# First gate and up columns ahead on ScalarE's queue, parameters behind x on SyncE

## The chip, the cores and the metric

The kernel runs on one core of one Trainium2 chip. The metric is the device time of one execution in microseconds (us). The core has four compute engines, TensorE (PE), VectorE (DVE), ScalarE (ACT) and GpSimd (POOL), and SyncE (SP), which here only issues DMAs. ScalarE can issue DMAs too. DMAs issued by SP and by ScalarE go through two queues onto the same 16 DMA engines.

## What is computed

The input x has 2048 tokens of 512 features, in bf16. It is normalised, and two blocks work on the result xn: a diagonal complex state-space layer and a gated feed-forward layer. Their sum with x is the output.

```python
xn  = layernorm(x)                                  # over the 512 features
dt  = exp(log_dt);  Lam_bar = exp(dt * (Lambda_re + 1j * Lambda_im))
Bu  = xn @ (((Lam_bar - 1) / Lam)[:, None] * (B_re + 1j * B_im)).T
h_t = Lam_bar * h_(t-1) + Bu_t                      # 2048 steps, 512 complex states
ssm = 2 * real(h @ (C_re + 1j * C_im).T) + xn * Dskip
ffn = (gelu(xn @ w_gate) * (xn @ w_up)) @ w_down    # 1376 hidden columns
out = x + ssm + ffn
```

The three parameter vectors log_dt, Lambda_re and Lambda_im have 512 values each.

## The kernel before

The tokens are worked in four blocks of 512, and a block in four tiles of 128 tokens. For each block TensorE multiplies the normalised, transposed tokens (XNT) with the gate and up columns (GU, L788), with B (BU, L731), and later adds up the feed-forward and state-space outputs (DN, L861 and L872). VectorE does the scan of the recurrence (CHAIN, L770) and much of the elementwise work; ScalarE does the gelu and takes results out of PSUM.

Instructions are not emitted in the order of the program text. Every operation is recorded with the tiles that it reads and writes, an estimated duration and an engine; a planner (`Sched.schedule`) then orders VectorE, ScalarE and GpSimd by due times. TensorE and SP keep the order in which operations are recorded. Operations handed to `S.pin` keep the order in which they are pinned, ahead of all others of their engine. Waits on semaphores follow from the tiles read and written, and from `after`.

The first block has a start of its own, and the change lies there:

- **Loads.** SP issues the four x tiles of the first block one by one (L494), then Lambda_re and Lambda_im, then the second piece of the gate and up columns (`ld_gu(1)`, columns 256 to 383), then B by two transposing DMAs (L483), then the rest. ScalarE issues log_dt, the first 256 gate columns and the first 256 up columns (L490 to L492), before it loads its first function table.
- **Parameters.** The tile PRMT is [128 x 128]: rows 0 to 3 hold log_dt, rows 4 to 7 Lambda_re, and from row 8 Lambda_im; `ld_param` (L473) repeats Lambda_im over rows 8 to 31. VectorE zeroes rows 32 to 63 and 64 to 127 by two memsets (L522, L523). One transpose on TensorE (`TR_par`, L631) turns the whole tile, so every row must hold numbers. It waits for all three parameter loads. ScalarE reads its result (L669 to L675).
- **Normalisation.** For each of the four tiles VectorE takes statistics (L538, L539), ScalarE or GpSimd forms the inverse root (L573 and L574, or L558 and L559), and VectorE centres and scales (L567 in three pieces for tile 0, L554 for the others). The order on VectorE is pinned: statistics of tiles 0 and 1, centring of tiles 0 and 1, statistics of tiles 2 and 3, centring of tiles 2 and 3.
- **TensorE.** Warm-up matmuls on constants (L890), the transposes of tile 0 (L597), the gate pieces of tile 0, the transposes of tile 1, the last gate piece (L621), then the up pieces of tile 0 and both for tile 1 (L621), the parameter transpose, and the third column group with tiles 2 and 3 (L788, L597, L621). ScalarE copies the transposes out of PSUM (L607). After these comes BU of block 0 (L731).

```python
S.pin(*st[0], *st[1], *ln[0], *ln[1], *st[2], *st[3], *ln[2], *ln[3])   # VectorE, LN_lead
evT = [TR_lead(0)]                                                      # TensorE
lead_piece(0, 0, (0,)); lead_piece(0, 1, (0,))
evT.append(TR_lead(1))
lead_piece(0, 2, (0,))
for g in range(3): lead_piece(0, g, (1,))
lead_piece(1, 0); lead_piece(1, 1)
TR_par()
```

Of the kernel before, what the change touches and what calls it, by code (L numbers as in the profile page):

```python
# [308 lines left out]
NT, NB, KD, KP, KF = 16, 4, 4, 4, 11  # L309
# [17 lines left out]
D_TINY = 90.0  # L327
# [3 lines left out]
def build(nc, ins, out):  # L331
    with ExitStack() as es:
        E = es.enter_context
        S = Sched(nc, es)
# [13 lines left out]
        WG = A.alloc("WG", [KD, F + 32], BF16)  # L348
# [3 lines left out]
        WGc = [Buf("WGc%d" % i, "wg", i, i + 1) for i in range(len(FCH))]  # L352
# [50 lines left out]
        HPI = A.alloc("HPI", [1], F32)  # L403
        LRE = A.alloc("LRE", [KP], BF16)
        LIM = A.alloc("LIM", [KP], BF16)
        PRMT = A.alloc("PRM", [128], BF16)
        PRM = [Buf("PRM%d" % i, "prm", i, i + 1) for i in range(5)]
        DTB = A.alloc("DTB", [KP], F32)
        PA_all = A.alloc("PA", [24, KP], F32)
        PA = ring(PA_all, "PA", 24)  # L410
# [38 lines left out]
        def V(fn, dur, r, w, tag="", after=(), slack=0.0):  # L449
            op = S.op("vector", fn, dur, r, w, tag, after)  # L450
            op.slack = slack
            return op
# [5 lines left out]
        POOL = lambda fn, dur, r, w, tag="": S.op("gpsimd", fn, dur, r, w, tag)  # L458
        PE = lambda fn, dur, r, w, tag="": S.op("tensor", fn, dur, r, w, tag)

        def load(dst, src, nbytes, writes, tag, queue="sync"):
            return S.dma(lambda e: e.dma_start(dst, src), nbytes, writes=writes, tag=tag, queue=queue)  # L462

        def ld_x(t0, n, queue="sync"):
            return load(X_all.ap[:, t0:t0 + n, :], x2[128 * t0:128 * (t0 + n), :].rearrange("(j p) d -> p j d", p=128),
                        n * 128 * 1024, X[t0:t0 + n], "ld_x", queue)

        def ld_w(W, Wc, src, ci, queue="sync"):
            f0, f1 = FCH[ci]
            return load(W.ap[:, :, f0:f1], src[:, f0:f1].rearrange("(k p) f -> p k f", p=128),  # L470
                        512 * (f1 - f0) * 2, [Wc[ci]], "ld_w", queue)

        def ld_param(i, nm, queue="sync"):  # L473
            src, r0, n = ins[nm].rearrange("(s p) -> s p", p=128), KP * i, 1
            dst = PRMT.ap[r0:r0 + KP, :]
            if i == 2:
                n = (32 - r0) // KP
                dst = PRMT.ap[r0:32, :]
                src = src.unsqueeze(0).broadcast_to([n, KP, 128])
            return S.dma(lambda e: e.dma_start(dst, src), 1024 * n, writes=[PRM[i]], tag="ld_" + nm, queue=queue, lat=2300.0)  # L480

        def ld_tr(dst, nm):
            return S.dma(lambda e: e.dma_start_transpose(dst.ap, ins[nm]), 4.0 * 1000 * 330, writes=[dst], tag="tr_" + nm,  # L483
# [2 lines left out]
        def ld_gu(ci):  # L486
            ld_w(WG, WGc, ins["B_w_gate"], ci)
            ld_w(WU, WUc, ins["B_w_up"], ci)

        prm0 = ld_param(0, "A_log_dt", "scalar")  # L490
        g0 = ld_w(WG, WGc, ins["B_w_gate"], 0, "scalar")
        u0 = ld_w(WU, WUc, ins["B_w_up"], 0, "scalar")  # L492
        for t in range(4):
            ld_x(t, 1)  # L494
        ld_param(1, "A_Lambda_re")
        ld_param(2, "A_Lambda_im")
        ld_gu(1)
        ld_tr(BBT[0], "A_B_re")
        ld_tr(BBT[1], "A_B_im")
# [6 lines left out]
        def late_loads():  # L506
# [12 lines left out]
              POOL(lambda e: e.memset(WD.ap[:, KF - 1, :], 0.0), 300, [], [WDc[1]], "pad"),  # L519
              *[POOL(lambda e, k=k: e.memset(HT[k].ap[:, KF - 1, :], 0.0), 300, [], [HTt[k][KF - 1]], "pad")  # L520
                for k in range(2)])
        S.pin(V(lambda e: e.memset(PRMT.ap[32:64, :], 0.0), D_TINY, [], PRM[3:4], "pad"),  # L522
              V(lambda e: e.memset(PRMT.ap[64:128, :], 0.0), D_TINY, [], PRM[4:5], "pad"),  # L523
              V(lambda e: e.memset(HPI.ap, 0.5 * math.pi), D_TINY, [], [HPI], "hpi"),
              V(lambda e: e.tensor_scalar(IDN.ap, IOT.ap, 0.0, None, ALU.is_equal), 550, [IOT], [IDN], "ident"))

        rstate = {"n": 0}
# [48 lines left out]
        def LN_lead():  # L576
            st = [stats(tt) for tt in range(4)]
            rs = {0: rsqrt_act(0)}
            ln = [[center_piece(g) for g in range(len(CUTS[0]))]]
            for tt in range(1, 4):  # L580
                if tt == 2:
                    rsqrt(RQt[0][tt], MVt[0][tt].ap[:, 1:2], [MVt[0][tt]], 1)
                else:
                    rs[tt] = rsqrt_act(tt)
                ln.append([center(tt)])
            S.pin(*st[0], *st[1], *ln[0], *ln[1], *st[2], *st[3], *ln[2], *ln[3])
            return rs

        def TR_lead(tt, after=()):
            banks = ((6, 7, 4), (5, 6), (6,), (7,))[tt]  # L590
            turns = CUTS[tt] if len(banks) > 1 else ((0, KD),)
            parts = [bank_part(bank, 0, 256 * (d1 - d0)) for bank, (d0, d1) in zip(banks, turns)]
            for g, (bank, (d0, d1)) in enumerate(zip(banks, turns)):
                def f(e, bank=bank, d0=d0, d1=d1):
                    ins_ = None
                    for dk in range(d0, d1):
                        ins_ = e.transpose(PSH[bank][:, 128 * (dk - d0):128 * (dk - d0) + 128], XN[tt].ap[:, 128 * dk:128 * dk + 128],  # L597
                                           IDN.ap)
                    return ins_
                S.op("tensor", f, 100 * (d1 - d0), [XN0p[g] if tt == 0 else XN[tt], IDN], [parts[g]], "T0", after)  # L600
                if tt == 0:
                    warm_pe(1, (64, 128, 128)[g], 3)
            ev = []
            for g, (d0, d1) in enumerate(CUTS[tt]):
                h, c0 = (g, 0) if len(banks) > 1 else (0, d0)
                pt = PSH[banks[h]][:, 128 * c0:128 * (c0 + d1 - d0)]
                ev.append(ACT(lambda e, d0=d0, d1=d1, pt=pt: e.activation(  # L607
                    XNT[0].ap[:, d0:d1, 128 * tt:128 * tt + 128], pt.rearrange("p (k t) -> p k t", k=d1 - d0), ACTF.Copy),
                    d_act(128 * (d1 - d0)), [parts[h]], [XNTp[tt][g]], "evT"))
            return ev  # L610
# [19 lines left out]
        def TR_par():  # L630
            PE(lambda e: e.transpose(PSH[7][:, 512:640], PRMT.ap, IDN.ap), 100, PRM + [IDN], [PPK], "Tp")  # L631

# [35 lines left out]
        def decay():  # L668
            exps = [ACT(lambda e: e.activation(DTB.ap, PP[0], ACTF.Exp), 200, [PPK], [DTB], "exp_dt")]  # L669
            for s in range(KP):  # L670
                exps.append(ACT(lambda e, s=s: e.activation(PA[RRr].ap[:, s:s + 1], PP[1][:, s:s + 1], ACTF.Exp,
                                                            scale=DTB.ap[:, s:s + 1]),
                                200, [PPK, DTB], [A.sub(PA[RRr], "RR_%d" % s, s)], "exp_a"))
            c = [ACT(lambda e: e.activation(LRE.ap, PP[1], ACTF.Copy), 200, [PPK], [LRE], "par"),
                 ACT(lambda e: e.activation(LIM.ap, PP[2], ACTF.Copy), 200, [PPK], [LIM], "par")]  # L675
            d = [V(lambda e: e.tensor_tensor(pa(TH), DTB.ap, LIM.ap, ALU.mult), D_TINY, [DTB, LIM], [PA[TH]], "th"),
                 V(lambda e: e.tensor_scalar(w16(0, 4), pa(TH), 1.0 / TWO_PI, None, ALU.mult), D_TINY, [PA[TH]], [W16p[0]], "w"),
                 V(lambda e: e.tensor_scalar(w16(4, 8), pa(TH), 512.0 / TWO_PI, None, ALU.mult), D_TINY, [PA[TH]], [W16p[1]], "w"),
                 V(lambda e: e.tensor_scalar(w16(8, 16), w16(0, 8), 0.25, None, ALU.add), D_TINY, W16p[0:2], W16p[2:4], "w"),
                 V(lambda e: e.tensor_copy(KI.ap, W16.ap), D_TINY, W16p, [KI], "w"),  # L680
                 V(lambda e: e.tensor_tensor(FRC.ap, W16.ap, KI.ap, ALU.subtract), D_TINY, W16p + [KI], [FRC], "w")]
            t3 = ACT(lambda e: e.activation(SC16.ap, FRC.ap, ACTF.Sin, scale=SIN_SCALE), 1480, [FRC], [SC16], "sin16")
            return exps, c, d, t3
# [214 lines left out]
        def preload(tag, fn=lambda e: e.preload_act_table(ACTF.Gelu_apprx_tanh)):  # L898
            op = ACT(fn, 1300, [], [], tag)
            op.silent = True  # L900
            return op

        ldln = preload("ld_ln", lambda e: e.preload_act_table_set("natural_log_exp_and_others"))
        rs = LN_lead()
        warm_pe(9)
        warm_pe(1, 256)
        evT = [TR_lead(0)]
# [4 lines left out]
        for g in range(3):  # L912
# [4 lines left out]
        exps, cps, dec, t3 = decay()  # L917
# [5 lines left out]
        lead_piece(2, 1)  # L923
        gelu0 = preload("ld_gelu")
        GATE["gelu"] = [gelu0]
        S.pin(prm0, g0, u0, ldln, *rs[0], *rs[1], *evT[0], *evT[1], *rs[3], exps[0], cps[1], *evT[2], *evT[3],
              *exps[1:], cps[0], gelu0)
        S.pin(*dec)
        for k in range(2):
# [95 lines left out]
```

## Time and profile before

| | |
|---|---|
| median of 3 runs | 178.77 us (178.7 to 179.14) |
| the profiled execution, its own time | 179.29 us |
| its span, first to last instruction | 177.5 us |
| busiest group on TensorE | GU, L788, 321 matmuls, 67.3 us |
| next | DN, L861, 183 matmuls, 38.8 us |
| busiest group on VectorE | scan, L770, 32 instructions, 38.5 us |
| DMA over the span | 12.38 MB, mean 70 GB/s |

Times in the profile are microseconds from the start of the span. In the chain of waits each line has a start, a length and what ran or was waited for; "ACTq" and "SPq" are the issue of DMAs by ScalarE and SP, "issue" is time in which the engine waited for nothing that the profile shows. In the order of time, a line has start, length, engine, line of the kernel, operation, output and input and a count; in brackets stands how long the engine was idle before it and what released it. A DMA issue is listed with its size and the time from issue to landing. The DMA engines' share of busy time counts 16 engines.

### The profile page before, as it was taken

How to read it: one execution, taken by the hardware profiler on the slowest of the kernel's cores; microseconds unless marked ns; L12 is line 12 of the kernel's file. 1: busy time of each engine (PE TensorE's matmuls, PEld its weight loads, DVE VectorE, ACT ScalarE, POOL GpSimd, SP SyncE). 2: the span in 40 equal slices, each digit the busy share in tenths (PEclk: the TensorE clock that was granted, in tenths of full speed). 3: DMA queues.
4: the chain of work that ended last, by engine and by line, in shares of the span. 5: the costliest groups of instructions: out<-in, count | busy, mean ns of one | idle time of the engine just before them, and what ended most of it. 6: DMA issues, size and time to landing. Idle time of an engine off the chain costs nothing.

```text
span 177.5 us, 2429 instructions
## 1 busy us (share of the span) xinstructions
PE 173.1 (98%) x874; PEld 82.0 (46%) x889; DVE 161.4 (91%) x250; ACT 103.7 (58%) x202; POOL 11.4 (6%) x24
## 2 busy tenths in 40 slices
PE   8899999999999999999999999999999999999994
PEld 2684444444444444444444444444444444444453
DVE  5899998998999989999989999899999999999731
ACT  4699998999999999487677600047867610000000
POOL 5100200000001600500000000000000000000000
PEclk9999999999999999999999999999999999999999
DMA  5999835995000022242000000110000000002021
GB/s 147 256 257 342 231 61 139 272 207 148 0 0 4 0 59 59 76 101 59 4 2 0 0 0 0 63 61 0 0 0 0 4 0 0 0 30 87 5 83 35
DMA packets 26345, 12.38 MB, mean 70 GB/s; under 512 B 17662, under 2 KB 26334, under 8 KB 26334
## 3 DMA queue, kind: packets, MB, share of 16 engines
q1 hardware_dynamic: 25270, 11.71, 26.2%
q10 hardware_dynamic: 1064, 0.53, 1.2%
q8 instruction: 7, 0.11, 0.3%
q14 instruction: 4, 0.03, 0.1%
HBM read 6.46 MB, written 2.10 MB: 48 GB/s over the span
## 4 chain that ended last, share of the span: by engine, by line
PE 94%; DMA 3%; issue 1%; ACTq 1%; DVE 0%
PE PS L788 37%; PE PS L861 21%; PE PS L872 16%; PE PS L731 15%; DMA arena<-in_B_w_up_dram 3%; PE PS L820 2%; PE PS L621 1%; PE PS L836 1%; ACTq L480 0%; PE PS L597 0%; ACTq L462 0%; DVE arena L879 0%; PE PS L631 0%
## 5 line engine op out<-in xcount | busy, mean ns | idle before, releaser
L788 PE MATMUL PS<-arena 128*128 128x512 bf16 (+2 forms) x321 | 67.3, 366 | 0.4
L788 PEld LDWEIGHTS PS<-arena 128*128 128x128 bf16 x328 | 31.1, 98 | 35.4 <-ACT arena L827 0.8
L861 PE MATMUL PS<-arena 128*128 128x512 bf16 (+2 forms) x183 | 38.8, 366 | 0.2
L770 DVE TENSOR_TENSOR_SCAN arena<-arena 128x512 bf16<-128x512 f32 x32 | 38.5, 1251 | 0.0
L872 PE MATMUL PS<-arena 128*128 128x512 bf16 (+2 forms) x136 | 28.6, 366 | 0.0
L731 PE MATMUL PS<-arena 128*128 128x512 bf16 x124 | 27.9, 379 | 0.2
L796 ACT ACTIVATE arena<-PS 128x512 bf16<-128x512 f32 x40 | 23.9, 598 | 6.2 <-PE PS L788 5.8
L861 PEld LDWEIGHTS PS<-arena 128*128 128x128 bf16 x187 | 17.9, 98 | 20.4
L798 ACT ACTIVATE arena<-PS 128x512 bf16<-128x512 f32 x40 | 24.0, 600 | 5.4 <-PE PS L788 5.3
L740 ACT ACTIVATE arena<-PS 128x512 bf16<-128x512 f32 x26 | 15.2, 600 | 19.3 <-PE PS L731 19.3
L872 PEld LDWEIGHTS PS<-arena 128*128 128x128 bf16 x136 | 13.0, 98 | 14.7
L731 PEld LDWEIGHTS PS<-arena 128*128 128x128 bf16 x128 | 12.5, 98 | 14.9
L800 DVE TENSOR_TENSOR arena<-arena 128x512 bf16<-128x512 bf16 x40 | 15.9, 419 | 3.0 <-ACT arena L798 2.8
L759 DVE TENSOR_TENSOR arena<-arena 128x4096 bf16<-128x4096 bf16 x8 | 18.3, 2285 | 0.1
L760 DVE TENSOR_TENSOR arena<-arena 128x4096 bf16<-128x4096 bf16 x8 | 18.3, 2284 | 0.0
L879 DVE TENSOR_TENSOR arena<-PS,arena 128x512 bf16<-128x512 f32 (+2 forms) x17 | 10.8, 650 | 6.7 <-PE PS L872 5.5
L850 DVE TENSOR_TENSOR arena<-arena 128x512 f32<-128x512 bf16 x16 | 10.6, 689 | 0.4
L761 DVE TENSOR_TENSOR arena<-arena 128x2048 bf16<-128x2048 bf16 x8 | 9.8, 1220 | 0.1
L646 ACT ACTIVATE arena<-arena 128x512 bf16<-128x512 bf16 x8 | 6.1, 804 | 2.5 <-POOL arena L639 2.5
L538 DVE BATCH_NORM_STATS2 arena<-arena 128x6 f32<-128x512 bf16 x8 | 5.2, 685 | 1.4 <-DMA arena<-in_A_x_dram 1.2
L849 DVE TENSOR_TENSOR arena<-arena 128x512 bf16<-128x512 bf16 x16 | 6.3, 419 | 0.0
L723 DVE SCALAR_TENSOR_TENSOR arena<-arena 128x512 bf16<-128x512 bf16 x8 | 5.7, 748 | 0.5 <-ACT arena L721 0.5
(76 smaller groups left out, 110.0 us busy)
## 6 DMA issues: line engine op xcount, KB each, us to landing
out_dram<-arena SPq DMA_DIRECT2D x15, 128.0 KB, 1.7
arena<-in_A_x_dram SPq DMA_DIRECT2D x3, 512.0 KB, 6.7
arena<-in_B_w_down_dram SPq DMA_DIRECT2D x1, 1280.0 KB, 6.7
arena<-in_B_w_gate_dram SPq DMA_DIRECT2D x2, 384.0 KB, 5.9
arena<-in_B_w_up_dram SPq DMA_DIRECT2D x2, 384.0 KB, 6.7
arena<-in_A_x_dram SPq DMA_DIRECT2D x4, 128.0 KB, 3.2
arena<-in_B_w_gate_dram ACTq DMA_DIRECT2D x1, 256.0 KB, 4.4
arena<-in_B_w_up_dram ACTq DMA_DIRECT2D x1, 256.0 KB, 5.1
```

What stands on the lines that cost most here:

```text
L731: ins_ = e.matmul(PS[bank][:, c0:c1], BBT[c].ap[:, dk, 128 * s:128 * (s + 1)], XNT[b].ap[:, dk, c0:c1], start=(dk == 0), stop=(dk == KD - 1))
L740: return ACT(lambda e: e.activation(ss.ap, PS[bank][:, :], ACTF.Copy), d_act(512), [BANK[bank]], [ss], "evBu", slack=1500.0)
L759: V(lambda e: e.tensor_tensor(TB.ap, ssb.ap, sin4, ALU.mult), d_dve_tt2x(4096), [ssb, SINT], [TB], tag, after=GATE["rot"])
L760: V(lambda e: e.tensor_tensor(TA.ap, ssb.ap, cos4, ALU.mult), d_dve_tt2x(4096), [ssb, COST], [TA], tag, after=GATE["rot"])
L770: V(lambda e, g=g, rb=rb, init=init: e.tensor_tensor_scan(g.ap, rb, g.ap, init, ALU.mult, ALU.add), d_dve_scan(512), [g, PA[RRr]] + ([CARc ...
L788: ins_ = e.matmul(PS[bank][0:m, c0:c1], W.ap[:, dk, 128 * ft:128 * ft + m], XNT[b].ap[:, dk, c0:c1], start=(dk == 0), stop=(dk == KD - 1))
L796: g = ACT(lambda e: e.activation(GG[kk].ap[0:m, :], PS[bg][0:m, :], ACTF.Gelu_apprx_tanh), d_act(512), [BANK[bg]], [GG[kk]], "gelu", after ...
L798: u = ACT(lambda e: e.activation(UPB[kk].ap[0:m, :], PS[bu][0:m, :], ACTF.Copy), d_act(512), [BANK[bu]], [UPB[kk]], "evU", slack=1500.0)
L800: h = V(lambda e: e.tensor_tensor(HTt[k2][ft].ap[0:m, :], GG[kk].ap[0:m, :], UPB[kk].ap[0:m, :], ALU.mult), d_dve_tt2x(512), [GG[kk], UPB[ ...
L861: ins_ = e.matmul(o_, HTt[k2][ft].ap[:, tok], WD.ap[:, ft, c0:c1], start=(ft == 0), stop=False)
L872: ins_ = e.matmul(o_, SSc[k3][s][c].ap[:, tok], CT[c][s].ap[:, c0:c1], start=False, stop=(s == KP - 1 and c == 1))
L879: V(lambda e, o_=o_, ko=ko: e.tensor_tensor(OUTB[ko].ap[:, c0:c1], o_, XD[ko].ap[:, c0:c1], ALU.add), d_dve_1x(c1 - c0), [part, XD[ko]], [ ...
```

## The change

All three parameter loads move to SP's queue, behind the four x tiles, as loads of four rows each. PRMT is zeroed in one memset over all 128 partitions, the first instruction of VectorE, and the parameter loads wait for it. ScalarE's queue begins with the gate columns; the first of these loads is made to wait for the memset, though it does not write that tile. The two memsets of rows 32 to 127 go.

```diff
-        PRM = [Buf("PRM%d" % i, "prm", i, i + 1) for i in range(5)]
+        PRM = [Buf("PRM%d" % i, "prm", i, i + 1) for i in range(3)]
...
-        def ld_w(W, Wc, src, ci, queue="sync"):
+        def ld_w(W, Wc, src, ci, queue="sync", after=()):
...
-        def ld_param(i, nm, queue="sync"):
-            src, r0, n = ins[nm].rearrange("(s p) -> s p", p=128), KP * i, 1
-            dst = PRMT.ap[r0:r0 + KP, :]
-            if i == 2:
-                n = (32 - r0) // KP
-                dst = PRMT.ap[r0:32, :]
-                src = src.unsqueeze(0).broadcast_to([n, KP, 128])
-            return S.dma(lambda e: e.dma_start(dst, src), 1024 * n, writes=[PRM[i]], tag="ld_" + nm, queue=queue, lat=2300.0)
+        def ld_param(i, nm):
+            return S.dma(lambda e: e.dma_start(PRMT.ap[KP * i:KP * i + KP, :], ins[nm].rearrange("(s p) -> s p", p=128)), 1024,
+                         writes=[PRM[i]], tag="ld_" + nm, lat=2300.0)
...
-        prm0 = ld_param(0, "A_log_dt", "scalar")
-        g0 = ld_w(WG, WGc, ins["B_w_gate"], 0, "scalar")
+        zero = V(lambda e: e.memset(PRMT.ap, 0.0), 110, [], PRM, "pad")
+        S.pin(zero)
+        g0 = ld_w(WG, WGc, ins["B_w_gate"], 0, "scalar", (zero,))
         u0 = ld_w(WU, WUc, ins["B_w_up"], 0, "scalar")
         for t in range(4):
             ld_x(t, 1)
-        ld_param(1, "A_Lambda_re")
-        ld_param(2, "A_Lambda_im")
+        for i, nm in enumerate(("A_log_dt", "A_Lambda_re", "A_Lambda_im")):
+            ld_param(i, nm)
         ld_gu(1)
...
-        S.pin(V(lambda e: e.memset(PRMT.ap[32:64, :], 0.0), D_TINY, [], PRM[3:4], "pad"),
-              V(lambda e: e.memset(PRMT.ap[64:128, :], 0.0), D_TINY, [], PRM[4:5], "pad"),
-              V(lambda e: e.memset(HPI.ap, 0.5 * math.pi), D_TINY, [], [HPI], "hpi"),
+        S.pin(V(lambda e: e.memset(HPI.ap, 0.5 * math.pi), D_TINY, [], [HPI], "hpi"),
...
-        S.pin(prm0, g0, u0, ldln, *rs[0], *rs[1], *evT[0], *evT[1], *rs[3], exps[0], cps[1], *evT[2], *evT[3],
+        S.pin(g0, u0, ldln, *rs[0], *rs[1], *evT[0], *evT[1], *rs[3], exps[0], cps[1], *evT[2], *evT[3],
```

The planner, given these, also puts a few instructions of VectorE around 17 us in another order: the eviction of the fifth BU bank (L739) comes ahead of a gate-up product (L800) and of the statistics of the second block, that product behind the centring of the second block (L554), and one small product of the parameters (L698) later. TensorE's order is the same, and so is ScalarE's apart from the load that has left it.

More of the change, by code (lines that the diff above doesn't have):

```diff
@@ L459, in build, with load @@
         PE = lambda fn, dur, r, w, tag="": S.op("tensor", fn, dur, r, w, tag)
-        def load(dst, src, nbytes, writes, tag, queue="sync"):
-            return S.dma(lambda e: e.dma_start(dst, src), nbytes, writes=writes, tag=tag, queue=queue)
+        def load(dst, src, nbytes, writes, tag, queue="sync", after=()):
+            return S.dma(lambda e: e.dma_start(dst, src), nbytes, writes=writes, tag=tag, queue=queue, after=after)
         def ld_x(t0, n, queue="sync"):
@@ L466, in ld_x @@
                         n * 128 * 1024, X[t0:t0 + n], "ld_x", queue)
-        def ld_w(W, Wc, src, ci, queue="sync"):
+        def ld_w(W, Wc, src, ci, queue="sync", after=()):
             f0, f1 = FCH[ci]
             return load(W.ap[:, :, f0:f1], src[:, f0:f1].rearrange("(k p) f -> p k f", p=128),
-                        512 * (f1 - f0) * 2, [Wc[ci]], "ld_w", queue)
-        def ld_param(i, nm, queue="sync"):
-            src, r0, n = ins[nm].rearrange("(s p) -> s p", p=128), KP * i, 1
-            dst = PRMT.ap[r0:r0 + KP, :]
-            if i == 2:
-                n = (32 - r0) // KP
-                dst = PRMT.ap[r0:32, :]
-                src = src.unsqueeze(0).broadcast_to([n, KP, 128])
-            return S.dma(lambda e: e.dma_start(dst, src), 1024 * n, writes=[PRM[i]], tag="ld_" + nm, queue=queue, lat=2300.0)
+                        512 * (f1 - f0) * 2, [Wc[ci]], "ld_w", queue, after)
+        def ld_param(i, nm):
+            return S.dma(lambda e: e.dma_start(PRMT.ap[KP * i:KP * i + KP, :], ins[nm].rearrange("(s p) -> s p", p=128)), 1024,
+                         writes=[PRM[i]], tag="ld_" + nm, lat=2300.0)
         def ld_tr(dst, nm):
```

## The prediction

> **What bounds the kernel now.** I read the page first, for which engine is full, then the chain of waits from its start, then the start of the kernel engine by engine in order of time, and last the DMA queues in short windows.
>
> The page's busy times:
>
> ```profile
> PE 173.1 (98%) x874; PEld 82.0 (46%) x889; DVE 161.4 (91%) x250; ACT 103.7 (58%) x202; POOL 11.4 (6%) x24
> PEclk9999999999999999999999999999999999999999
> ```
>
> TensorE is full, at the full granted clock. What moves the end is therefore what moves the point from which it runs without a gap. The chain of waits, in order of time (start, length, what), shows that point:
>
> ```profile
> 0.72 0.56 ACTq L480
> ...
> 1.31 0.40 ACTq L462
> ...
> 1.74 5.09 DMA arena<-in_B_w_up_dram
> 6.83 0.05 issue
> 6.88 1.51 PE PS L621 x24
> ...
> 175.27 0.29 DVE arena L879
> ```
>
> From 6.88 us to the end every step but the last is TensorE's own work. Before 6.88 the chain is ScalarE's queue: log_dt issued (0.56), gate columns (0.40), up columns, whose landing 5.09 us after the issue lets TensorE go. This alone says that to take log_dt away brings the end forward. So the next view is TensorE's stretch just before:
>
> ```profile
> 4.13 0.52 PE L890 MATMUL PS<-const-bfloat16-1.0 128*128 128x512 bf16 x2
> 4.96 0.23 PE L597 MATMUL PS<-arena 128*128 128x128 bf16 x1 [0.31 <-DVE arena L567]
> ...
> 6.20 0.40 PE L621 MATMUL PS<-arena 128*128 128x128 bf16 x4
> 6.88 1.51 PE L621 MATMUL PS<-arena 128*128 128x128 bf16 x24 [0.28 <-DMA arena<-in_B_w_up_dram]
> ```
>
> The wait for the up columns is only 0.28 us. Take it away and TensorE is held by its work at 4.96 to 6.60, the transposes of x tiles 0 and 1 and the gate pieces, and these wait for VectorE:
>
> ```profile
> 2.76 0.69 DVE L538 BATCH_NORM_STATS2 arena<-arena 128x6 f32<-128x512 bf16 x1 [1.04 <-DMA arena<-in_A_x_dram]
> 3.49 0.18 DVE L539 BATCH_NORM_AGGREGATE arena<-arena 128x2 f32<-128x6 f32 x1
> 3.79 0.69 DVE L538 BATCH_NORM_STATS2 arena<-arena 128x6 f32<-128x512 bf16 x1
> 4.52 0.18 DVE L539 BATCH_NORM_AGGREGATE arena<-arena 128x2 f32<-128x6 f32 x1
> 4.62 0.76 DVE L567 TENSOR_SCALAR arena<-arena 128x128 bf16<-128x128 bf16 x3
> ```
>
> Here lies the second chain. In the order written for VectorE the statistics of x tile 1 (3.79) stand ahead of the centring of tile 0 (4.62), so that both tiles wait for tile 1's load. It was issued on SP at 1.19 and its window gives 2.6 us to landing, 3.77 by the landing records: statistics start 0.02 us later. Tile 1 is just in time, with 0.28 us in hand until TensorE feels it.
>
> How x loads and weight loads share the DMA engines shows in the third x tile, issued at 1.64, between the gate columns (1.31) and the up columns (1.74). First its issue, then the queues from 2.9 to 3.6 us (queue 10 is ScalarE's, queue 1 SP's; packets, MB, share of the engines):
>
> ```profile
> arena<-in_A_x_dram SPq DMA_DIRECT2D x1, 128.0 KB, 3.8
> ```
>
> ```profile
> q10 hardware_dynamic: 167, 0.09, 57.2%
> q1 hardware_dynamic: 9, 0.01, 3.0%
> ```
>
> Tile 2 takes 3.8 us where tile 1 takes 2.6 and tile 0 takes 2.0. From 2.9 to 3.6 the engines are not full (busy 0.60), and yet SP's queue, with tile 2 issued at 1.64 and tile 3 at 2.10, moves 9 packets, 7 of them tile 1's last. Tile 2's own begin near 3.6. So it does not share with the gate columns: it stands behind them, in the order of issue, whatever its queue.
>
> **The change part by part.**
>
> *VectorE's start.* Two memsets of 0.11 us (L522, L523) become one over all partitions, 64 words wide as those: about 0.11, from 0.79 to 0.90. VectorE idles 1.04 us before 2.76; nothing.
>
> *ScalarE's queue.* The log_dt issue (0.56) goes. The gate issue now waits for the memset; behind it on ScalarE stand the up issue, the table load (2.29, 1.28 long) and the first Ln (3.77, which has 0.20 of idle before it). A wait of ScalarE on VectorE ended 0.10 after the releaser (3.49 + 0.18 = 3.67 to 3.77), so the gate issue starts at about 0.98 to 1.00 instead of 1.31: 0.33 earlier. The up issue follows at 1.41 instead of 1.74. The table load ends near 3.2, earlier than now.
>
> *The order of the loads.* SP's issues stay: x tiles at 0.72, 1.19, 1.64, 2.10. Today's order is x0, log_dt, x1 (1.19), gate (1.31), x2 (1.64), up (1.74), x3. The new one is x0, gate (0.98), x1 (1.19), up (1.41), x2, x3. By the end of the issue it is the same: gate 0.98 + 0.40 = 1.38, x1 at 1.60. The gate columns (256 KB) have passed tile 1, which now stands where tile 2 stood: right behind the gate and just ahead of the up columns. Tile 2 landed at 1.64 + 3.8, 5.46 by the landing records. With the gate 0.33 earlier the like place lands at 5.13; with also one x tile less ahead (128 KB at the 347 GB/s of 4.2 to 5.0 us, 0.38) at 4.75. I take the middle, 4.95, as the engines were partly idle in that stretch and so the second saving is not whole. Tile 1 comes 4.95 - 3.77 = 1.18 us later. The bounds: 3.77, if it is not held up at all, and 5.46, tile 2's landing as it is.
>
> The Trainium skill (DMA: Bandwidth & Descriptors, "Queues, rings and completion order") speaks against this: each engine goes round its queues packet by packet, by which tile 1 would share with the gate from its first packet. The empty stretch from 2.9 to 3.6 disagrees; the rule's outcome is the first rival below.
>
> *The gain.* The up columns land earlier, by 0.33 to 0.7 us. Worth at most the 0.28 us of TensorE's wait, as the pieces end at 6.60.
>
> *The loss.* Statistics of tile 1 at 4.97, and everything behind on VectorE, TensorE and ScalarE keeps its distances: centring of tile 0 at 5.80, first transpose at 6.14, gate pieces ending at 6.60 + 1.18 = 7.78, up columns long there. TensorE's gap-free run begins at 7.78 instead of 6.88: +0.90. What is late next? Tile 2 now stands behind the up columns and lands with tile 3, by 6.8 at the latest as the bytes are the same; its statistics are due at 5.71 + 1.18 = 6.89 and tile 3's at 7.9, so they add nothing. TensorE has no gap later in which to win anything back.
>
> *Parameters on SP.* SP issues three copies of 4 rows instead of one of 4 (0.37) and one of 24 (0.90): between 3 x 0.37 and 3 x 0.56 against 1.36 with the gap, so the second gate and up columns are issued 0.25 earlier to 0.3 later than 3.95. They took 3.5 us and are needed at 8.28 + 0.9: hidden. The transpose pieces of B behind them (4.97, 4.9 us) are needed at 12.48: hidden. The parameters land behind x3, as two of them do today (7.04 and 7.25 by the landing records); their transpose ran at 8.22. Cover 0.9 us, and more with the shift. Were the cover gone, each tenth would cost a tenth.
>
> *VectorE's order near 17 us.* The planner puts the fifth BU eviction ahead of a product (0.42) and of the statistics of the second block, the product behind their centring, and one 0.15 product of parameters later. No instruction is added. Bounds 0 to 0.15; I take 0, since the product's next user, ScalarE at 24.87, is 0.6 us behind, and VectorE is waited for by TensorE nowhere in the chain but at its end.
>
> *Sum.* -0.28 + 1.18 = +0.90. The profiled execution took 179.29, its span 177.5 and 1.79 around it; it would give 180.19. It lies 0.52 above the median of the runs, 178.77, which gives 179.67.
>
> **The rivals.**
>
> *Tile 1 is not held up; not slower.* If queues share packet by packet, each of tile 1's 8 packets per engine (38 packets at 89.0% of 16 engines in 0.12 us: 45 ns) waits for one of the gate's (403 at 84.4% in 0.8 us: 27 ns): 8 x 27 = 0.22 us. It lands at 3.99, TensorE's run begins at 6.60 + 0.22 = 6.82: 178.71, and 178.49 where nothing is lost. It decides below a landing at 4.05 (3.77 + 0.28). For it: gate packets and tile 2's do mix after 3.6. Against: the empty 0.7 us. By the rule of the Trainium skill named above this is the outcome.
>
> *The gate does not pass tile 1.* If the memset's signal frees ScalarE 0.2 us later than I have it, the order stays as it is, and only log_dt's place is won: up to 0.28, 178.5. For it: only 0.2 us separates the issues. Against: waits of 0.10.
>
> *The array cools.* TensorE's warm-up ends at 4.65 and its next work comes at 6.14 instead of 4.96. At the start its 512-column matmuls stood 0.43 apart for 3.9 us, later 0.215. Should a gap of 1.5 us bring that back for as long, half of 3.9 is lost: 179.67 + 1.95 = 181.6. For it: the gap is five times longer. Against: the present gaps of 0.31 and 0.28 cost nothing. The Trainium skill (TensorE: Matmul & The Clock Gate, Part 1) has the clock fall only after an idle window of some 3.4 us, by which this would not happen; no run here shows it yet.
>
> **How the numbers follow.** Forecast: tile 1 behind the gate, 0.62. Tile 1 not held up, 0.22. Gate does not pass, 0.07. Cooling, 0.06. Anything else 0.03. A measurement of this kernel can tell about 0.3% from no change, 0.54 us. The forecast's own bounds: above, tile 1 at 5.46, 1.69 late; below, the hold that the gate put on SP's queue (its first packets at 2.6, tile 2's at 3.6, so 1.0) less the 0.33 by which it begins earlier, 0.67 late. That is 178.77 - 0.28 + 0.67 to 1.69: 179.2 to 180.2. It passes 0.54 us where tile 1 lands after 4.59, nine times in ten. Slower: 0.56 + 0.06 + 0.01 = 0.63. Same: 0.06 + 0.20 + 0.06 = 0.32. Faster: 0.02 + 0.01 + 0.02 = 0.05, as no row offers more than 0.28. The range takes in both first rivals and the upper bound with 0.2 of spread: 178.4 to 180.4.
>
> **What would show it.** Right: statistics of tile 1 near 4.97 with a wait of about 1.2 us for the x load; the first transpose near 6.14; no wait for the up columns; the run of 24 up and gate pieces starting near 7.8; busy time of every engine unchanged, the span 0.9 longer. Wrong: statistics of tile 1 before 4.1, the gate's issue after 1.2, or matmuls 0.43 apart behind 6.1. The parameters' transpose waiting for a DMA would break the step that hides them.

## The result, and the profile after

The changed kernel is slower. Over 12 runs its median is 179.74 us, against 178.91 us for the kernel before (12 runs, 178.7 to 179.22). The ratio, which like every ratio below compares means and not medians, is 1.0075 with a 95% interval of 1.0048 to 1.0102: 180.28 against 178.94 us, a loss of 1.34 on the mean.

The interval is wide because the changed kernel has two kinds of execution: seven lie between 179.60 and 179.76, five between 180.99 and 181.28, and none between. The kernel before has one kind: its executions in all runs, over 60, lie between 178.70 and 179.64. So there are two losses to explain: some 0.8 us in every execution, and 1.4 us more in some.

| | before | after |
|---|---|---|
| median | 178.91 | 179.74 |
| profiled execution, its own time | 179.29 | 179.71 |
| its span | 177.5 | 177.9 |
| PE busy | 173.1 | 173.2 |
| DVE busy | 161.4 | 161.3 |

No engine has more to do. The chain of waits of the changed kernel, from its start (start, length, what), shows what has moved:

```profile
0.72 0.39 SPq L462
...
1.18 3.44 DMA arena<-in_A_x_dram
...
4.64 0.70 DVE arena L532
...
5.37 0.18 DVE arena L533
5.55 0.21 DVE arena L561
...
5.81 0.23 PE PS L591
...
7.14 1.65 PE PS L615 x28
```

Line numbers are six lower than before, by the lines that left the kernel. The up columns are gone from the chain. In their place stands the load of x tile 1, issued on SP at 1.18 and landing 3.44 us later, and from there the path runs over VectorE's statistics and centring to TensorE's first transpose. VectorE in the order of time has the same wait:

```profile
3.62 0.18 DVE L533 BATCH_NORM_AGGREGATE arena<-arena 128x2 f32<-128x6 f32 x1
4.64 0.69 DVE L532 BATCH_NORM_STATS2 arena<-arena 128x6 f32<-128x512 bf16 x1 [0.84 <-DMA arena<-in_A_x_dram]
```

Tile 0 is ready at 3.80, and VectorE then idles 0.84 us for tile 1. ScalarE's queue issues the gate columns at 0.95, ahead of tile 1, and the up columns at 1.40. While the gate columns move, SP's queue gets next to nothing. From 2.5 to 3.0 us (packets, MB, share of the 16 engines; queue 10 is ScalarE's):

```profile
q10 hardware_dynamic: 158, 0.08, 79.8%
q1 hardware_dynamic: 2, 0.00, 0.7%
```

### The profile page after: what moved, and what is told of

The parts are those of the page before. It is cut to its first block, busy times and chain, and to the rows that moved or that the text cites. A ratio compares the mean times of both kernels' runs of the same rounds, so it can differ in the third digit from the quotient of the medians.

```text
span 177.9 us, 2428 instructions
## 1 busy us (share of the span) xinstructions
PE 173.2 (97%) x874; PEld 82.0 (46%) x889; DVE 161.3 (91%) x249; ACT 103.7 (58%) x202; POOL 11.4 (6%) x24
## 4 chain that ended last, share of the span: by engine, by line
PE 95%; DMA 2%; DVE 1%; issue 1%; SPq 0%
PE PS L782 37%; PE PS L855 21%; PE PS L866 16%; PE PS L725 15%; PE PS L814 2%; DMA arena<-in_A_x_dram 2%; PE PS L615 2%; PE PS L830 1%; PE PS L591 1%; DVE arena L532 0%; SPq L462 0%; DVE arena L873 0%; DVE arena L561 0%; DVE arena L533 0%; PE PS L884 0%
```

## The experiments

Four theories are set against each other. A: tile 1 is late because the gate's load was issued ahead of it; in its strict form, a load stands behind every load issued before it. B: the loss comes from the memset, the wait on it or the parameter loads. C: the longer executions are those in which TensorE's clock is low behind a longer gap. D: in these a load or another wait is later still.

**The order alone.** The kernel before, with log_dt moved behind the two weight loads on ScalarE and nothing else changed.

```diff
-        prm0 = ld_param(0, "A_log_dt", "scalar")
         g0 = ld_w(WG, WGc, ins["B_w_gate"], 0, "scalar")
         u0 = ld_w(WU, WUc, ins["B_w_up"], 0, "scalar")
+        prm0 = ld_param(0, "A_log_dt", "scalar")
...
-        S.pin(prm0, g0, u0, ldln, ...
+        S.pin(g0, u0, prm0, ldln, ...
```

> The kernel before with one change: on ScalarE's queue log_dt is issued behind the gate and up columns, so the gate is issued at 0.72, ahead of x tile 1 (1.19). Two memsets, parameters and SP's queue as before. Theory A (a load stands behind every load issued before it, whatever its queue): statistics of tile 1 start 0.8 to 1.2 us later than 3.79, near 4.6 to 5.0, first transpose near 5.8 to 6.1, time 179.4 to 180.0, with some executions near 181.1 as in the changed kernel. Rival B (the loss comes from the wait for the memset or from the three parameter loads on SP, not from the order of gate and tile 1): neither is in this kernel, so 178.5 to 178.9 and no second group of times.

Median 179.68 us, ratio 1.0057 (1.0035 to 1.0080), seven executions at 179.60 to 179.84 and two at 181.04 and 181.25. VectorE has the wait of the changed kernel:

```profile
4.58 0.69 DVE L538 BATCH_NORM_STATS2 arena<-arena 128x6 f32<-128x512 bf16 x1 [0.63 <-DMA arena<-in_A_x_dram]
```

To issue the weight loads earlier, the gate ahead of tile 1, makes both losses by itself; the memset, the wait on it and the parameters on SP are not needed for either.

**The change without the order.** The changed kernel, with the gate waiting for a later signal, so that it is issued at 1.17 with its issue ending behind that of tile 1.

```diff
-        g0 = ld_w(WG, WGc, ins["B_w_gate"], 0, "scalar", (zero,))
+        g0 = ld_w(WG, WGc, ins["B_w_gate"], 0, "scalar", (pool[2],))   # GpSimd's third memset
```

> The changed kernel with one change: the gate load waits for GpSimd's third memset (done near 1.14) instead of VectorE's first (0.91), so it is issued near 1.25, just behind x tile 1 (1.18). Theory A: tile 1 is in time again, statistics at 3.8 to 3.9, up columns landing near 6.8, time 178.6 to 179.0, and the executions near 181 are gone. Rival B (memset, parameters on SP): these are all still there, so 179.6 to 181.3 as in the changed kernel.

Median 178.83 us, 178.75 to 179.37 in 11 runs, ratio 0.9994 (0.9986 to 1.0003): as the kernel before. To issue the gate 0.22 us later makes the kernel 0.9 us faster by the medians. The up columns landed at 6.18, earlier than expected. VectorE in the order of time:

```profile
3.66 0.18 DVE L534 BATCH_NORM_AGGREGATE arena<-arena 128x2 f32<-128x6 f32 x1
3.76 0.66 DVE L533 BATCH_NORM_STATS2 arena<-arena 128x6 f32<-128x512 bf16 x1
```

Tile 1 is there when VectorE is done with tile 0, and the wait has gone. Everything else in the change, the single memset and three parameter loads on SP, costs nothing that could be measured.

**The kernel before once more**, for a second trace, as the profiled execution of before took 0.38 us more than its median.

> The kernel before once more, for a second trace, since the profiled execution shown took 179.29 against a median of 178.91. If the wait of 0.28 for the up columns belongs to that execution and not to the usual one: TensorE's run of up pieces begins near 6.4 to 6.6, with no wait for the up columns, and the time is 178.8 to 179.0. If the wait is there always: again near 6.9.

It took 178.93 us, span 177.1. Its chain of waits:

```profile
1.19 2.67 DMA arena<-in_A_x_dram
...
3.88 0.71 DVE arena L538
...
5.05 0.23 PE PS L597
...
6.38 1.65 PE PS L621 x28
```

The up columns are not in this chain: the pieces run on without a break from 6.38. In this execution, which lies at the median, the path to TensorE already runs over tile 1; the wait of 0.28 us for the up columns belonged to the slower execution that was shown. Against this trace the changed kernel's run of 28 pieces starts 7.14 - 6.38 = 0.76 us later, the span is 0.8 longer, and the times differ by 179.71 - 178.93 = 0.78.

**Half the gate ahead.** The changed kernel, with the first gate load cut in two, of which only columns 0 to 127 go ahead of tile 1.

```diff
-        FCH = [(0, 256), (256, 384), ...
+        FCH = [(0, 128), (128, 256), (256, 384), ...
         g0 = ld_w(WG, WGc, ins["B_w_gate"], 0, "scalar", (zero,))
+        g1 = ld_w(WG, WGc, ins["B_w_gate"], 1, "scalar")
```

> The changed kernel with the first gate load cut in two: columns 0 to 127 issued at 0.95 ahead of x tile 1, columns 128 to 255 behind it at about 1.4, then the up columns near 1.85. Ahead of tile 1 stand as many pieces as in the changed kernel (512, one for each row), of half the bytes. If tile 1 is held by bytes ahead of it: the hold of 0.77 (landing 3.86 in the second trace of the kernel before, 4.62 in the changed one) halves, statistics of tile 1 near 4.25. If it is held by the number of pieces, as where a load's pieces are listed one by one before the next load's turn: statistics near 4.6 as in the changed kernel. If it is not held by the gate at all: near 3.85.

```profile
4.11 0.69 DVE L534 BATCH_NORM_STATS2 arena<-arena 128x6 f32<-128x512 bf16 x1 [0.41 <-DMA arena<-in_A_x_dram]
```

Tile 1 lands at 4.09, 0.23 later than the 3.86 of the trace above, where the whole gate made it 4.62, 0.76 later. The number of pieces ahead was the same, so it is not their number alone that sets the hold. Fewer bytes shorten it, to about a third, by one trace each, where a half was expected. The median is 179.20 us, ratio 1.0007 (0.9997 to 1.0016), and all ten executions lie between 179.09 and 179.51: the second loss is gone too.

**Gate and up columns ahead.** The changed kernel with tile 1 held on SP until GpSimd's second iota is done; SP's later loads move back with it by about 0.4 us.

```diff
-        for t in range(4):
-            ld_x(t, 1)
+        ld_x(0, 1)
+        ld_x(1, 1, after=(iotj,))
+        ld_x(2, 1)
+        ld_x(3, 1)
```

> The changed kernel with one change: x tile 1 waits on SP for GpSimd's second iota (done near 1.63), so it is issued near 1.65 to 1.7 instead of 1.18, by the end of the issue behind the up columns too. Theory A (a load stands behind every load issued before it): tile 1 takes the place that tile 2 has in the changed kernel, landing near 5.5 to 5.6 instead of 4.62, 3.9 us after its issue; time 180.5 to 180.8 where the clock is granted early, more in other executions. Rival (a load takes its own time from its issue, 2.6 to 3.4 as tile 1 has taken so far): landing at 4.3 to 5.1, time 179.4 to 180.2.

Tile 1 was issued at 1.67 and landed 3.43 us later, at 5.10, before the up columns (5.41 by the landing records), though these were issued first. Three executions took 179.89 to 180.33 us and three 181.18 to 181.81, ratio 1.0088 (1.0054 to 1.0122); that the median, 180.75, lies where theory A had it comes from mixing the two kinds. Theory A in its strict form has failed: it asked for 5.5 to 5.6, and for 180.5 at the least. The landing lies at the upper end of the rival's range, and 3.43 us is what tile 1 took in the changed kernel (3.44). But no fixed time of its own fits all the traces: it took 2.67 ahead of the gate and 2.91 behind half of it. The two queues in two windows, 2.6 to 3.4 us and 3.6 to 4.4 us:

```profile
q10 hardware_dynamic: 492, 0.25, 112.3%
```

```profile
q10 hardware_dynamic: 306, 0.16, 64.1%
q1 hardware_dynamic: 134, 0.12, 44.9%
```

In the first, while the gate moves, SP's queue has no packet at all. In the second tile 1 and the up columns go side by side. Counted packet by packet, tile 1's first one starts here behind all 512 of the gate and 63 of the up columns, and in the changed kernel behind 232 of the gate's 512 (276 to 388 in its other traces). So the tile is shut out for a stretch and shares after it. What ends the stretch, the moment when descriptors are made or something else, these runs do not tell.

**VectorE's written order.** The changed kernel with the centring of tile 0 ahead of the statistics of tile 1.

```diff
-            S.pin(*st[0], *st[1], *ln[0], *ln[1], *st[2], ...
+            S.pin(*st[0], *ln[0], *st[1], *ln[1], *st[2], ...
```

> The changed kernel with VectorE's written order changed in one place: centring of x tile 0 ahead of the statistics of tile 1. If both tiles wait for tile 1's load only by that order, tile 0 is centred from about 4.45 (its root is done at 4.43) and its first transpose runs near 4.8 instead of 5.81, with tile 1 landing as late as before; but tile 1's statistics then wait for VectorE until about 5.2, so the transposes of tile 1 move from 6.8 to about 7.2 and the time is 179.7 to 180.2. If the late start came from something else than tile 1's load, the first transpose stays near 5.8.

The first transpose ran at 4.82 and the transposes of tile 1 at 7.20. Two executions took 180.09 and 180.14, two 181.70 and 181.71; ratio 1.0101 (1.0051 to 1.0150). So it is VectorE's order that made the centring of tile 0 wait for the load of tile 1, and to change it alone makes the kernel slower, by 0.4 us where the second loss is absent: tile 1's statistics come later (5.15). The run does not show that tile 0 could not carry TensorE further. The gate pieces of tile 0 ran only here:

```profile
6.93 0.38 PE L615 MATMUL PS<-arena 128*128 128x128 bf16 x4 [1.29 <-ACT arena L601]
```

They wait for ScalarE's copy of tile 0's transposes, and ScalarE's own pinned order puts that copy behind the inverse root of tile 1 (6.09 and 6.42 in the chain of waits). That order was left as it was, and no run changes both.

**The second loss: a longer warm-up.** The changed kernel with 11 warm-up matmuls in place of 9.

```diff
-        warm_pe(9)
+        warm_pe(11)
```

> The changed kernel with 11 warm-up matmuls of 512 columns instead of 9 (0.43 us each at the start, so the warm-up ends near 5.3 to 5.7 instead of 4.97, still before the first transpose at 5.81). Theory C (the executions near 181.1 are those in which TensorE's clock is low behind the longer gap): the group near 181.1 is gone, all executions near 179.7. Rival D (in those executions tile 1 lands later still, or another wait is longer): both groups stay, near 179.7 and 181.1.

> The changed kernel with 11 warm-up matmuls once more, for more executions, since 5 without a long one can be chance when 5 of 12 were long before. Theory C (clock): again all near 179.7 to 179.8. Rival D: some near 181.1.

Medians 179.76 (5 runs, 179.68 to 180.01) and 179.88 us (6 runs, 179.65 to 179.97); ratios 1.0046 (1.0033 to 1.0059) and 1.0043 (1.0026 to 1.0059). None of 11 executions was near 181, against 5 of 12 without. The 0.8 us stays. (Both traces are of executions in which TensorE reached full speed early, at 3.68 and 4.49 us, so that the last warm-up matmuls ran faster and a gap of 0.99 and 0.77 us is seen all the same.)

**The same from the other side.** The kernel before, with 7 warm-up matmuls in place of 9 and every load where it was.

> The kernel before with 7 warm-up matmuls of 512 columns instead of 9: the warm-up ends near 3.8 instead of 4.65, so the gap ahead of the first transpose (4.96) is about 1.1 instead of 0.31, with every load where it was. Theory C: a share of the executions, or all, is 1.2 to 1.6 us longer, near 180.3. Rival D: 178.9 as before, one group, since no load moves.

Five executions at 178.82 to 178.93, seven at 180.27 to 180.85; ratio 1.0053 (1.0025 to 1.0081). A gap ahead of the first transpose makes the second kind of execution even with no load moved. In its trace, of an execution of 180.81, the gap was 0.85 us where 1.1 was expected, and the 28 pieces are slow:

```profile
4.97 0.29 PE L597 MATMUL PS<-arena 128*128 128x128 bf16 x1 [0.85 <-DVE arena L567]
6.60 3.19 PE L621 MATMUL PS<-arena 128*128 128x128 bf16 x28
```

**The changed kernel, more traces.**

> The changed kernel once more, for a second trace. Statistics of tile 1 near 4.6 in either case. Where the time is near 179.7, TensorE's 28 pieces take 1.74 as before; where it is near 181.1, theory C expects them to take 2.7 to 3.2 with the same loads and the same VectorE times, rival D a later tile 1 or another wait.

> The changed kernel, a third trace, to catch one of its longer executions. Theory C: in an execution near 181.1 the 28 pieces take 2.7 to 3.2 us instead of 1.74, with VectorE's times as in the others. Rival D: the pieces take 1.74 and tile 1 or another wait is later by 1.4.

> As the run before it: a fourth trace of the changed kernel, with the same two expectations for an execution near 181.1.

They took 179.75, 181.47 and 179.88 us. The second is one of the long executions. First its VectorE and then its TensorE, in the order of time:

```profile
4.76 0.69 DVE L532 BATCH_NORM_STATS2 arena<-arena 128x6 f32<-128x512 bf16 x1 [0.96 <-DMA arena<-in_A_x_dram]
```

```profile
5.93 0.29 PE L591 MATMUL PS<-arena 128*128 128x128 bf16 x1 [0.96 <-DVE arena L561]
...
7.55 2.98 PE L615 MATMUL PS<-arena 128*128 128x128 bf16 x28
```

Against it the TensorE line of the first trace of the changed kernel:

```profile
7.05 1.74 PE L615 MATMUL PS<-arena 128*128 128x128 bf16 x28
```

Tile 1 is as late as in the fourth trace (statistics at 4.80), of an execution of 179.88. But the 28 pieces take 2.98 us in place of 1.74, one every 0.106 us where it is 0.062 otherwise. That is the pace of the start: a 512-column warm-up matmul took 0.43 us there, four times 0.106, and such matmuls take half of it, 0.215, later. By the chains of waits the stretch from the first transpose to the third column group takes 4.66 us (5.93 to 10.59) against 3.03 in the fourth trace (5.97 to 9.00); with the start 0.04 earlier that is the whole 1.59 between the two executions. The trace also records when the throttle grants a clock: full speed at 10.17 us here, at 4.89 in the first trace and at 3.76 in the fourth.

What the gap is to be counted from is the end of the warm-up at the slow pace: 4.97 us with nine matmuls, 4.12 with seven, and with eleven 5.83, an estimate from 4.97 and twice 0.43. So counted it is 0.84 us in the changed kernel, 0.77 with log_dt moved and 0.85 with the short warm-up, and these have long executions: 6 of 15, 2 of 9 and 7 of 12. It is 0.31 with half the gate ahead, less than 0.2 with eleven matmuls and less than 0.1 in the kernel before, and these have none: 0 of 10, 0 of 11 and none of over 60.

## Why the prediction was right or wrong

The direction, the place and the sum held for the first loss: +0.90 forecast, and 0.83 between the medians, 0.78 between two executions without the second loss. On the mean the loss is 1.34, as the forecast left the second loss out. Two terms were wrong, with opposite signs.

*The order of the loads.* The gate passed tile 1 as worked out: issued at 0.95 where 0.98 was forecast, and both one-part kernels show that this order alone is enough, and that without it there is no loss.

*The loss of 1.18* was too large. Tile 1 landed at 4.62, not 4.95, 0.85 later than in the execution shown and 0.76 later than in the second trace. In the four traces of the changed kernel it landed at 4.62 to 4.78. Of the two ways to reckon from tile 2, the one with both savings whole (4.75) comes close to these; what failed is the step to the middle (4.95), by which the saving of one x tile less ahead would not be whole. Why it was whole is open. That the gate landed at 5.69 in the execution shown and at 4.43 here does not settle it: in the second trace of the kernel before the gate landed at 4.91, and tile 2 still at 5.40. The lower bound of 4.44 was below the measured value.

*The gain of 0.28* was not there. The wait for the up columns was taken from the one profiled execution, which took 0.38 us more than the median. In the second trace there is no such wait, and the path runs over tile 1. That the sum came out close is luck in part, as the two cancel: 1.18 - 0.28 against 0.76 - 0.

*The hidden parts* held. The memset, the parameters on SP and the earlier eviction near 17 us are all in the kernel with the gate behind, at ratio 0.9994. The product of L800 that moved with the eviction keeps its place ahead of the statistics there, so that part was not run alone; but in the changed kernel's chain no step of VectorE stands between the centring of tile 0 and the last addition.

*Tile 1 not held up*, with 0.22 the likeliest rival, failed: it wanted a landing at 3.99. It had the two queues take turns row by row, one packet of the trace each. That fits 3.6 to 4.4 us of the kernel with both loads ahead (306 packets beside 134) and not 2.5 to 3.0 us here (158 beside 2). The rule of the Trainium skill (DMA: Bandwidth & Descriptors, "Queues, rings and completion order"), that an engine goes round its queues packet by packet, is not refuted by this: a packet of that page holds 9 to 17 descriptors as a rule and 64 at most, so that many rows of one load can go before the other queue has its turn. No run here shows where such packets end.

*The array cools* got 0.06, and happened in five of the first twelve executions. The mechanism was named and the step to its chance was wrong. It asked whether a gap can take away a clock already granted. The clock had not been granted yet: in the four traces of long executions full speed comes only at 9.53 to 10.17 us. The row of the granted clock, from which I took full speed throughout, could not tell this. The sign that I had set for being wrong, the slow pace behind 6.1 us, did appear in these. Its price was 1.95; measured are 1.4 between the groups. The idle rule that I quoted was not the one that applies. The other rule of the same part of the Trainium skill (TensorE: Matmul & The Clock Gate, Part 1) does: full speed comes after a busy window of about 3.4 us, and the window runs freely against the kernel. That agrees with a warm-up that suffices in some executions and not in others (a gap of 0.85 us after 3.4 us of warm-up: seven of twelve long), and with two more warm-up matmuls sufficing in all eleven. The clock records agree too. In the other ten traces full speed was granted between 3.68 and 5.32 us, and the grants last 174.08 us after these and 170.67 after the late ones, 3.41 apart. As an estimate, windows of 3.41 us laid back from the four late grants put the gap inside the window before (from 2.70 to 3.35 us, to 6.12 to 6.76), which held 0.77 us of idling or more and granted nothing, while the windows that end at the early grants held up to 0.5.

The second-named rival, that the gate does not pass tile 1, failed by the issue times. Made on purpose, it is the better kernel, at 178.83.

No kernel of these beats the kernel before clear of noise; the gate behind tile 1 equals it with the simpler parameter loads.

## What to carry to other kernels

At the start of a kernel, order loads by when their first reader needs them, over all queues together: a weight load that passed a small activation load by 0.2 us at the issue held it up by 0.8 here. Before taking a wait from a trace as something to be won, see whether that execution is the usual one by its own time against the median; a second trace costs little. When something delays TensorE's first work, lengthen the warm-up to reach it, and look for two groups of times, which a median hides.

## What the runs showed of the hardware

The row of the granted clock does not show the slow start: the trace holds no clock record from before the first grant. In the execution of 181.47 us it reads full speed throughout:

```profile
PEclk9999999999999999999999999999999999999999
```

and yet the 28 pieces stand 0.106 us apart. The distance between matmuls of one form is the sign to go by.

The hold of one queue by the other was not proportional to the bytes: 256 KB ahead held tile 1 by 0.76 us, 128 KB by 0.23, by one trace each.
